# Attention and MLP on one core: the first loads of x, keys and wq divided anew over the SP and ACT queues

## The chip, the core and the metric

One core of one Trainium2 chip. The metric is device microseconds of one execution. The profile's span runs from the first to the last instruction and is about 1.8 us shorter than that time (1236.3 us for a run of 1238.15 us). "Us" in the text is microseconds from the start of the span unless a duration is meant.

## The reference, cut to what matters

```python
def reference(A_x, A_k_cache, A_v_cache, A_wq, A_wo, B_x, B_w1, B_b1, B_w2, B_b2):
    xn = layernorm(A_x)                                  # 2048 x 512, bf16
    q = (xn @ A_wq)                                      # 32 heads of 128
    p = softmax(einsum("bhqd,bhkd->bhqk", q, k_cache) * 128 ** -0.5)
    s = einsum("bhqk,bhkd->bhqd", p, v_cache) @ A_wo
    h = relu(xn @ B_w1 + B_b1) ** 2                      # 512 -> 1792
    g = silu(h @ B_w2 + B_b2)
    return A_x + s * g
```

## The kernel before

TensorE works almost without a break for 1220 us. Nothing of that can begin before four small things have happened: a tile of x (128 rows) has been normalized, transposed and projected to queries of head 0, and the keys of head 0 have been transposed. The kernel therefore starts with loads on two queues, SP's and ACT's, and a hand-ordered beginning.

The loads before the change (`AC` is ACT; a load without a queue goes to SP):

```python
    t_x0 = S.emit_dma(AC, partial(_dma, out=x_ln[P // 2:P, 0, :], in_=A_x[0, P // 2:P, :]), sl_x0)
    t_xl[0] = S.emit_dma(SP, partial(_dma, out=x_ln[0:P // 2, 0, :], in_=A_x[0, 0:P // 2, :]),
                         sl_xl[0])          # x tile 0 in two halves of 64 rows
    ln_load(0, 1, AC)                       # x tile 1, 128 KB, rows of 1 KB
    load_k0(0)                              # first keys: half of head 0's, 256 KB, rows of 2 KB
    fill_wq(0, AC)                          # head 0's wq, 128 KB, rows of 256 bytes
    load_k0(1)                              # second keys
    ...
    ln_load(0, 2, SP); ln_load(0, 3, SP); fill_wq(1); load_v0(0); load_v0(1)
    fill_k(1); fill_wq(2); fill_v(1); load_w1(0)
    for i, k in enumerate([2, 3, 12, 18, 26, 34]):
        at(k, partial(load_w1, i + 1))      # the other w1 loads, at step k of the attention
```

The order of the beginning. Every engine runs its own part of this list in this order:

```python
    warm_up(36)            # TensorE: 36 matmuls on zeros
    k0_transpose(0)        # TensorE: 8 transposes of the first keys
    k0_copy(0)             # ScalarE: copy of the result
    ln_bn(0, 0)            # VectorE: statistics of x tile 0
    ln_rstd(0, 0, eng=DV)  # VectorE, then POOL: the scale factor of tile 0
    ln_bn(0, 1)            # VectorE: statistics of x tile 1
    ln_scale(0, 0)         # VectorE: tile 0 scaled (xn_t)
    first_transpose(0)     # TensorE: tile 0's transposes
    k0_transpose(1)        # TensorE: 8 transposes of the second keys
    bias_rows()
    k0_copy(1)
    ln_rstd(0, 1, eng=DV)
    first_copy(0)
    bias_copy()
    first_proj(0)          # TensorE: queries of head 0 for tile 0
    ln_scale(0, 1)
    first_evac(0)
    first_transpose(1)
    gen_scores(0)          # TensorE: the first scores
    ...                    # cut: from here on TensorE has work all the time
```

The softmax here doesn't subtract the row's maximum and nothing guards it: scores larger than these inputs give would overflow.

## Time and profile before

| | |
|---|---|
| median of the first 3 runs | 1238.32 us (1238.1 to 1238.4) |
| all 42 runs of this kernel | median 1238.49 us; 35 below 1239, mean 1238.44; 7 from 1239.25 to 1240.57 |
| TensorE busy | 1231.2 of 1236.3 us |
| first scores start | 8.05 us |
| x tile 1 lands, first keys land | 5.10, 4.71 us |

The prediction below shows the lines of this profile. They are read so: in a timeline row, start and duration, engine, line, operation, what it writes `<-` what it reads, number of instructions merged; in brackets how long the engine was idle before and what ended that. In the chain of work that ended last there are start, duration and what the end of the execution hung on at that time.

### The profile page before, as it was taken

The page shows a single profiled execution, that of the slowest core. Times are in us where ns is not written, and L with a number is a line of the kernel's source. Part 1 is how long each engine was busy: PE and PEld are TensorE (multiplying, and loading weights), DVE is VectorE, ACT ScalarE, POOL GpSimd, SP SyncE. Part 2 cuts the span into 40 slices and gives each one's busy share as a digit, 9 for nine tenths or more (in the row PEclk, how much of TensorE's full clock was granted, in tenths as well). Part 3 has the DMA queues.
Part 4 walks back from the last instruction along what each step waited for, and adds up shares of the span by engine and source line. Part 5 has one row for each costly group of instructions (what it writes and reads, how often), then busy time and mean ns, then how long its engine had stood idle before and what let it go on. Part 6 is the DMA issues. An engine that isn't in the chain of part 4 may idle for free.

```text
span 1236.3 us, 26936 instructions
## 1 busy us (share of the span) xinstructions
PE 1231.2 (100%) x11885; PEld 818.7 (66%) x11885; DVE 472.5 (38%) x953; ACT 1053.7 (85%) x1044; POOL 31.9 (3%) x73
## 2 busy tenths in 40 slices
PE   9999999999999999999999999999999999999999
PEld 7666666666666666666666666666666666666666
DVE  4453323244435332334444532333344333324333
ACT  7888888888888888888888888888888888888885
POOL 1010000000002000000000200000000000000000
PEclk9999999999999999999999999999999999999999
DMA  9999997777879797878779978788779799878771
GB/s 213 203 243 194 186 178 134 131 143 142 141 151 170 143 160 129 138 140 144 133 133 170 172 138 144 141 148 133 133 145 148 146 154 158 137 134 147 146 123 31
DMA packets 686884, 185.41 MB, mean 150 GB/s; under 512 B 673552, under 2 KB 685584, under 8 KB 686768
## 3 DMA queue, kind: packets, MB, share of 16 engines
q1 hardware_dynamic: 684592, 179.56, 80.8%
q0 software_dynamic: 1424, 3.81, 1.3%
q8 instruction: 94, 1.54, 0.5%
q10 hardware_dynamic: 752, 0.33, 0.1%
q14 instruction: 22, 0.18, 0.1%
HBM read 96.60 MB, written 2.10 MB: 80 GB/s over the span
## 4 chain that ended last, share of the span: by engine, by line
PE 99%; DVE 0%; DMA 0%; ACTq 0%; issue 0%; DVEq 0%
PE psO L157 38%; PE psA L152 36%; PE psF L152 25%; DMA x_ln<-in_A_x_dram 0%; PE psA L157 0%; DVE out_t L165 0%; PE psF L196 0%; DVE tmp_t L175 0%; PE psO L152 0%; DVE st_t L200 0%; DVE xn_t L171 0%; ACTq L208 0%; PE psO L196 0%; DVE xnT L179 0%; DVE b1f L179 0%
## 5 line engine op out<-in xcount | busy, mean ns | idle before, releaser
L161 ACT ACTIVATE pT<-psA 128x1024 bf16<-128x1024 f32 x1024 | 1043.5, 1023 | 163.6 <-PE psA L152 118.3
L157 PEld LDWEIGHTS psO<-v_sb,pT 128*128 128x128 bf16 x8192 | 547.9, 98 | 240.2 <-issue 12.5
L157 PE MATMUL psO<-v_sb,pT 128*128 128x129 bf16 x8192 | 631.2, 220 | 0.0
L152 PE MATMUL psA<-qt_sb,kT 128*128 128x512 bf16 x2032 | 604.4, 379 | 0.0
L179 DVE COPY o_un<-psO 128x258 f32<-128x258 f32 x256 | 97.3, 421 | 399.6 <-PE psO L157 398.9
L152 PE MATMUL psF<-xnT,wq_sb 128*128 128x512 bf16 (+1 forms) x520 | 168.8, 374 | 0.1
L152 PE MATMUL psF<-wo_all,oT 128*128 128x512 bf16 x480 | 163.6, 379 | 0.0
L152 PEld LDWEIGHTS psA<-qt_sb,kT 128*128 128x128 bf16 x2032 | 157.0, 98 | 0.0
L179 DVE CAST qt_sb<-psF 128x512 bf16<-128x512 f32 (+1 forms) x130 | 87.9, 676 | 97.1 <-PE psF L152 97.1
L165 DVE TENSOR_TENSOR o_bf<-o_un,rden 128x512 bf16<-128x512 f32 x128 | 88.6, 692 | 4.6 <-DVE rden L183 0.3
L152 PEld LDWEIGHTS psF<-xnT,wq_sb 128*128 128x128 bf16 x520 | 50.3, 98 | 59.8 <-DVE xnT L179 0.2
L171 DVE TENSOR_SCALAR r_t<-psF,b1f 128x512 bf16<-128x512 f32 x56 | 42.0, 750 | 117.5 <-PE psF L152 117.5
L152 PEld LDWEIGHTS psF<-wo_all,oT 128*128 128x128 bf16 x480 | 46.9, 98 | 56.4
L152 PE MATMUL psF<-xnT,w_sb 128*128 128x512 bf16 x224 | 77.1, 379 | 0.0
L152 PE MATMUL psF<-w_sb,h2T 128*128 128x512 bf16 x224 | 74.1, 379 | 0.0
L152 PEld LDWEIGHTS psF<-w_sb,h2T 128*128 128x128 bf16 x224 | 21.9, 98 | 26.4
L152 PEld LDWEIGHTS psF<-xnT,w_sb 128*128 128x128 bf16 x224 | 21.9, 98 | 26.4
L165 DVE TENSOR_TENSOR z_t<-psF,b2bc 128x512 f32<-128x512 f32 x16 | 11.1, 692 | 67.2 <-PE psF L152 67.2
L165 DVE TENSOR_TENSOR acc<-psF,acc 128x512 f32<-128x512 f32 x28 | 19.3, 688 | 30.0 <-PE psF L152 30.0
L208 POOL DMA_DIRECT2D out_dram<-out_t x12 | 6.7, 555 | 891.0 <-DVE out_t L165 891.0
L165 DVE TENSOR_TENSOR h2T<-r_t 128x512 bf16<-128x512 bf16 x56 | 23.8, 425 | 1.9
L183 DVE RECIPROCAL rden<-o_un 128x4 f32<-128x4 f32 x128 | 22.9, 179 | 4.4
(47 smaller groups left out, 164.3 us busy)
## 6 DMA issues: line engine op xcount, KB each, us to landing
v_sb<-in_A_v_cache_dram SPq DMA_DIRECT2D x127, 512.0 KB, 4.7
wq_sb<-in_A_wq_dram SPq DMA_DIRECT2D x127, 128.0 KB, 3.0
wo_all<-in_A_wo_dram SPq DMA_DIRECT2D x4, 1024.0 KB, 6.3
w_sb<-in_B_w_dram SPq DMA_DIRECT2D x14, 256.0 KB, 4.6
oT<-o_bf SPq DMA_TRANSPOSE x128, 3.9
x_t<-in_A_x_dram POOLq DMA_DIRECT2D x16, 128.0 KB, 3.6
kT<-in_A_k_cache_dram SPq DMA_TRANSPOSE x127, 4.5
x_ln<-in_A_x_dram SPq DMA_DIRECT2D x14, 128.0 KB, 4.2
```

The lines of the kernel that those rows point to most:

```text
L152: return e.matmul(out, lhsT, rhs, start=start, stop=stop)
L157: return e.matmul(out, lhsT, rhs, start=start, stop=stop, skip_group_check=True)
L161: return e.activation(out, in_, func, bias=bias, scale=scale)
L165: return e.tensor_tensor(out, in0, in1, op)
L171: return e.tensor_scalar(out, in0, scalar1=scalar1, scalar2=scalar2, op0=op0, op1=op1)
L179: return e.tensor_copy(out, in_)
L183: return e.reciprocal(out, in_)
L208: return e.dma_start(out, in_)
```

## The change

The intent: x tile 1, which the chain of work waits for, gets the place right behind tile 0 on SP; the first keys move to ACT in its stead; head 0's wq follows the second keys on SP.

```diff
-    def load_k0(b):
+    def load_k0(b, eng=SP):
...
-            SP, partial(_dma, out=kT[:, NSL - 1, b * n * P:(b + 1) * n * P],
+            eng, partial(_dma, out=kT[:, NSL - 1, b * n * P:(b + 1) * n * P],
...
-    ln_load(0, 1, AC)
-    load_k0(0)
-    fill_wq(0, AC)
+    ln_load(0, 1, SP)
+    load_k0(0, AC)
     load_k0(1)
+    fill_wq(0)
```

## The prediction

> **What bounds the kernel now.** I first read the busy shares on the page, then the chain of work that ended last, then busy time by stretch, and only then the first 8 us instruction by instruction.
>
> ```profile
> PE 1231.2 (100%) x11885; PEld 818.7 (66%) x11885; DVE 472.5 (38%) x953; ACT 1053.7 (85%) x1044; POOL 31.9 (3%) x73
> ...
> PE 99%; DVE 0%; DMA 0%; ACTq 0%; issue 0%; DVEq 0%
> ```
>
> TensorE is busy 1231.2 of 1236.3 us, and 99% of the chain is its own. The stretches say where it isn't:
>
> ```profile
> 0.00:8.05 8.05, 5.92 (x66) 5.18 (x66) 3.58 (x12) 3.50 (x4) 3.16 (x14) 1.00 0.80 202
> 8.05:20.00 11.95, 11.88 (x177) 10.23 (x176) 5.50 (x17) 9.78 (x12) 2.08 (x5) 1.00 1.10 215
> 20.00:620.00 600.00, 600.00 (x5748) 396.56 (x5747) 232.88 (x467) 516.16 (x511) 12.49 (x28) 1.00 0.87 159
> 620.00:1220.00 600.00, 600.00 (x5792) 398.26 (x5790) 223.25 (x446) 522.47 (x519) 11.66 (x24) 1.00 0.80 142
> ```
>
> Columns: stretch, length, then PE, PEld, DVE, ACT and POOL busy, granted clock, DMA share, GB/s. From the first scores at 8.05 us to 1220 us, TensorE is never out of work for more than 0.07 us in all. The change touches only the first 8 us, where 8.05 - 5.92 = 2.1 us lie idle (and 3.65 us of the "busy" are warm-up matmuls on zeros). So the question is only when the stream of scores starts; a shift there should reach the end one to one. The chain up to there:
>
> ```profile
> 0.73 0.58 ACTq L208
> 1.31 0.04 issue
> 1.35 3.75 DMA x_ln<-in_A_x_dram
> 5.10 0.02 issue
> 5.12 0.69 DVE st_t L200
> 5.81 0.33 DVE xn_t L171
> 6.14 0.05 issue
> 6.19 0.40 PE psF L196 x4
> ```
>
> Columns: start, us, what. The load is x tile 1, issued second on ACT, landing at 5.10. Its statistics hold up tile 0: VectorE runs in program order, the statistics of tile 1 stand before the scaling of tile 0 (xn_t), and the scale factor was there already:
>
> ```profile
> 4.46 0.57 POOL L165 TENSOR_TENSOR rstd<-ve_t,mhalf 128x1 f32<-128x1 f32 x1 [1.75 <-DVE ve_t L171]
> 4.75 0.45 PEld L196 LDWEIGHTS psO<-ident,kT 128*128 128x128 bf16 x8 [0.30 <-DMA kT<-in_A_k_cache_dram]
> 4.76 0.62 PE L196 MATMUL psO<-ident,kT 128*128 128x128 bf16 x8
> 5.12 0.69 DVE L200 BATCH_NORM_STATS2 st_t<-x_ln 128x6 f32<-128x512 bf16 x1 [0.75 <-DMA x_ln<-in_A_x_dram]
> ```
>
> POOL is done at 4.46 + 0.57 = 5.03; the scaling of tile 0 starts at 5.73. That 0.7 us is all that an earlier tile 1 can give before POOL is the limit.
>
> **What the Trainium skill says.** "Perfetto Trace Analysis", section "DMA Instruction — HWDGE (DVE, Sync)": the descriptor generator (DGE) is one block shared by the issuing sequencers, locked for exclusive use, and the profiled time of an issue includes the wait for the lock. The trace agrees in part: x tile 1's issue on ACT took 0.85 us beside 0.56 for the keys issued at the same moment on SP, but other issues overlap. "DMA: Bandwidth & Descriptors", section "Issuing engines are not separate DMA queues": loads from SP and ACT run on the same 16 engines and interleave, so dividing them saves only issue time. So the number of queues is not the gain here; the order is. The same page, section "Queues, rings and completion order": each engine takes turns between its queue rows, packet by packet. That would let x tile 1 share with the keys from the start, and the trace contradicts it. Packets in 2.8 to 3.4 us, then 3.4 to 3.8 us:
>
> ```profile
> q1 hardware_dynamic: 55, 0.11, 86.7%
> ...
> q1 hardware_dynamic: 45, 0.08, 60.0%
> q10 hardware_dynamic: 14, 0.01, 19.0%
> ```
>
> q1 is SP's row, q10 ACT's. ACT's row is empty from 2.8 to 3.4 although x tile 1 was issued at 1.35 and its 0.85 us issue was over at 2.20: its descriptors came only after those of the first keys. "PSUM — Partial Sum Buffer", section "Engine vs sequencer instructions": the VectorE queue is strict FIFO. The trace agrees: the scaling of tile 0, ready at 5.03, waits until the statistics are through at 5.73.
>
> **The change part by part.** No byte, no instruction is added or removed; three transfers change queue.
>
> 1. x tile 1: from second on ACT to second on SP, still issued near 1.36. The 256 KB of the first keys, issued on SP at 1.36, started packets at about 2.5 and hold the generator nearly 1 us; tile 1's packets began at about 3.45 and landed 1.65 us later. On SP I expect it to have the place that the keys had: packets from 2.5, and landing near 2.5 + 1.65 = 4.15 (estimate). The statistics can then start at 4.21 + 0.15, about 4.38, and are through near 5.0; the scaling is then limited by POOL's 5.03, so starts at 5.07 instead of 5.73: 0.66 us.
>
> 2. First keys (half 0): from second on SP to second on ACT, behind x tile 1 in the generator. Landed at 1.36 + 3.4 = 4.75. Half the bytes of the keys (128 against 256 KB) now go ahead, worth about half of the keys' 0.97 us: +0.4 (estimate), 5.1 to 5.2. The eight key transposes stand before tile 0's transposes in TensorE's order and take 0.45 us of issue (their row above). So tile 0's transposes start at the later of 5.07 + 0.46 = 5.53 (the trace has 5.73 to 6.19) and 5.15 + 0.45 = 5.60, instead of 6.19: 0.6 us. ScalarE's first copy of the keys moves from 5.42 to about 5.8, its second starts at 6.8 instead of 7.07. No cost.
>
> 3. Second keys: stay on SP as its third load, with the same bytes ahead of them over both queues, so landing as before at 1.98 + 3.8 = 5.8. Their transposes ran at 6.42; now they are wanted at about 5.83. Just in time.
>
> 4. Head 0's wq: from ACT (issued 2.23, landed 2.23 + 4.4 = 6.6) to SP behind the keys, issued near 2.4. It is in front of x tiles 2 and 3 and no longer takes turns with them, so 6.4 to 6.6. The first projection started at 7.19, with 0.57 us from the copy xnT (6.62) to it; at 6.60 it now finds wq barely there. I take 0 to 0.1 us as lost.
>
> 5. x tiles 2 and 3, wq 1 and the values are issued one issue (0.43 us) later on SP, but they queue for DMA anyway (x tile 2 took 4.4 us from issue to landing), so they land as before within 0.2 us. Tile 2 (6.8) is wanted at 7.2, wq 1 (7.7) at 8.5, the first values (3.87 + 5.1 = 9.0) at 9.77 - 0.6 = 9.15: the last has only 0.15 us to spare, and may cost 0 to 0.2 us.
>
> 6. ScalarE has one load issue less (0.45 us), so its 1.28 us table load starts near 2.3 instead of 2.71 and ends near 3.6. Off the path: the first copy waits for TensorE.
>
> Sum: -0.6 from steps 1 and 2, +0.05 for wq, +0.05 for values: about -0.5 us, or 0.04% of 1238.32. Predicted 1237.8 us.
>
> **The rivals.** (a) ACT wins the tie. Both queues issue near 1.35, and the keys won on SP although ACT's issue began 10 ns earlier, so SP seems preferred. If the keys on ACT go first after all, x tile 1 again lands at 5.1 and nothing changes: 1238.3. (b) ACT's row itself is slow. Tile 1's late packets could be the second load on ACT being late for its own sake, not standing behind the keys. Then the keys get that lateness: 2.1 us from issue to first packets and about 1.9 us to the end, landing at 5.5 to 5.8, and the keys take the place of x as the wait: tile 0's transposes at 6.0 to 6.2, a gain of 0 to 0.2, so 1238.1 to 1238.3. For it: ACT's half of tile 0 also began later (0.25 us behind SP's). Against it: the empty row in 2.8 to 3.4 fills just when the keys' first engines are through. (c) wq or values become the new bound, wholly: each could swallow up to 0.3 us, result 1238.0. (d) All is hidden: if something else fed TensorE later, the shift would be lost. Against it: no idle of any size between 8.05 and 1220 us, and ScalarE has 0.60 us of idle before the first exponentials.
>
> **Range and chances.** Chain limit at best: 1238.32 - 0.7 = 1237.6; steps as worked out 1237.8; rivals a and b 1238.3; keys later than in b could make it worse by 0.2 or so. The three runs differ by 0.3 us among themselves, half of which I add on each side. Range 1237.3 to 1238.6. A change of 2% would be 25 us, three times the whole start, so faster 0.01, same 0.98, slower 0.01.
>
> **What would show it.** Right: the first wait of VectorE for the second load falls from 0.75 us to nearly 0; statistics of tile 1 at about 4.4; the scaling at 5.1, released by POOL; the key transposes at 5.1 to 5.2; tile 0's transposes at 5.6; the first scores at about 7.5 instead of 8.05; and the rest of the span unchanged. ACT's row empty until about 3.0 and then filled with 2 KB packets. Wrong: tile 1 still near 5.1 (rival a); keys past 5.3 with TensorE waiting for them (rival b); the first projection or the first value matmuls waiting for a DMA (rival c); first scores earlier but the end unchanged (rival d). A difference of more than 1 us would mean that something outside the start moved.

## The result, and the profile after

The median of 6 runs is 1238.28 us (1237.81 to 1240.16), against 1238.30 for 6 runs of the kernel before. The ratio of the fast runs is 1.0001, with a 95% interval of 0.9988 to 1.0014: the same. (A ratio here is the mean time of one kernel's fast runs over that of the other's of the same rounds, so not quite the ratio of the quoted medians.) Leaving out the upper group, which had 2 of the 6 runs after and 1 of the 6 before, the means are 1238.09 and 1238.25.

The chain of work that ended last, of the changed kernel, its first 8 us (start, duration, what):

```profile
1.34 4.60 DMA kT<-in_A_k_cache_dram
5.94 0.05 issue
5.99 0.62 PE psO L196 x8
6.61 0.22 PE psF L196 x4
```

Where the chain before had x tile 1 until 5.10, it now has the first keys until 5.94. The timeline of the changed kernel shows both sides of it:

```profile
3.62 0.69 DVE L200 BATCH_NORM_STATS2 st_t<-x_ln 128x6 f32<-128x512 bf16 x1 [3.62 <-DMA x_ln<-in_A_x_dram]
...
4.63 0.68 DVE L200 BATCH_NORM_STATS2 st_t<-x_ln 128x6 f32<-128x512 bf16 x1
4.81 0.57 POOL L165 TENSOR_TENSOR rstd<-ve_t,mhalf 128x1 f32<-128x1 f32 x1 [2.10 <-DVE ve_t L171]
5.41 0.41 DVE L171 TENSOR_SCALAR xn_t<-x_ln,mv_t,rstd 128x512 bf16<-128x512 bf16 x1
...
5.99 0.62 PE L196 MATMUL psO<-ident,kT 128*128 128x128 bf16 x8 [0.99 <-DMA kT<-in_A_k_cache_dram]
...
8.30 1.05 PE L157 MATMUL psA<-qt_sb,kT 128*128 128x128 bf16 x16
```

The same two steps of TensorE in the kernel before (tile 0's transposes, first scores):

```profile
6.19 0.40 PE L196 MATMUL psF<-ident,xn_t 128*128 128x128 bf16 x4 [0.81 <-DVE xn_t L171]
...
8.05 1.05 PE L157 MATMUL psA<-qt_sb,kT 128*128 128x128 bf16 x16
```

The wanted part happened: the statistics of tile 1 no longer wait for their load (the second line has no bracket), and the scaling of tile 0 starts when POOL is through, at 5.38. It comes at 5.41 instead of 5.73. But TensorE waits for the keys until 5.99, and tile 0's transposes stand behind them. The first scores start at 8.30, a quarter of a microsecond later than before. From there to the end every weight load of TensorE is 0.25 us later than its counterpart of the kernel before, and the profiled run took 1238.41 us, 0.26 more than the one of before.

So this one profile shows a loss of a quarter of a microsecond, and the runs of the lower group a gain of 0.16 us. Both cannot be the whole story; what differs from run to run had to be found.

### The profile page after: what moved, and what is told of

The parts are those of the page before. It is cut to its first block, busy times and chain, and to the rows that moved or that the text cites. A ratio compares the mean times of both kernels' runs of the same rounds, so it can differ in the third digit from the quotient of the medians.

```text
span 1236.6 us, 26729 instructions
## 1 busy us (share of the span) xinstructions
PE 1220.5 (99%) x11678; PEld 818.6 (66%) x11885; DVE 472.3 (38%) x953; ACT 1053.5 (85%) x1044; POOL 31.9 (3%) x73
## 4 chain that ended last, share of the span: by engine, by line
PE 98%; issue 1%; DMA 0%; DVE 0%; ACTq 0%; DVEq 0%
PE psO L157 38%; PE psA L152 35%; PE psF L152 25%; DMA kT<-in_A_k_cache_dram 0%; PE psA L157 0%; DVE out_t L165 0%; PE psF L196 0%; PE psO L196 0%; DVE tmp_t L175 0%; PE psO L152 0%; ACTq L208 0%; DVE xnT L179 0%; DVE xn_t L171 0%; DVE b1f L179 0%; PE psA L196 0%
## 5 line engine op out<-in xcount | busy, mean ns | idle before, releaser
L152 PE MATMUL psA<-qt_sb,kT 128*128 128x512 bf16 x1840 | 563.0, 379 | 10.1
L152 PE MATMUL psF<-xnT,wq_sb 128*128 128x512 bf16 (+1 forms) x508 | 165.7, 374 | 0.3
```

The lines of the kernel that those rows point to most:

```text
L152: return e.matmul(out, lhsT, rhs, start=start, stop=stop)
```

## The experiments

Twelve runs followed, the changed kernel once more and eleven new ones. Kernels are compared only within the same rounds. Since each profile is one execution, I kept a table of the same few moments for all of them (the sections below refer to it; times in us, "L" and "U" count runs of the lower and the upper group):

| kernel | first keys: queue, landed | x tile 1 landed | tile 0 scaled | first scores | profiled run | L / U | before in the same call, mean of L |
|---|---|---|---|---|---|---|---|
| before | SP, 4.71 | 5.10 | 5.73 | 8.05 | 1238.15 | 35 / 7 | |
| changed | ACT, 5.94 | 3.90 | 5.41 | 8.30 | 1238.41 | 4 / 2 | 1238.25 |
| changed, again | ACT, 4.92 | 3.61 | 5.16 | 7.65 | 1238.19 | 5 / 0 | 1238.49 |
| all on SP | SP, 5.73 | 3.95 | 5.00 | 9.23 | 1239.33 | 2 / 3 | 1238.49 |
| both keys on ACT | ACT, 5.73 | 4.14 | 5.45 | 8.44 | 1238.54 | 4 / 1 | 1238.49 |
| before, scaling first | SP, 4.73 | 5.14 | 5.28 | 8.18 | 1238.28 | 4 / 1 | 1238.49 |
| changed, w1 later | ACT, 6.05 | 3.74 | 5.42 | 8.41 | 1238.55 | 3 / 2 | 1238.53 |
| before, w1 later | SP, 4.75 | 5.11 | 5.75 | 8.23 | 1238.34 | 4 / 1 | 1238.53 |
| changed, 18 warm-ups | ACT, 5.93 | 3.75 | 5.29 | 9.43 | 1240.36 | 0 / 5 | 1238.53 |
| changed, x first | ACT, 5.25 | 3.76 | 5.30 | 8.05 | 1238.16 | 5 / 0 | 1238.53 |
| second keys wait | ACT, 4.69 | 3.60 | 5.15 | 9.86 | 1240.54 | 0 / 4 | 1238.48 |
| whole tiles | SP, 4.36 | 3.57 | 5.20 | 7.74 | 1237.85 | 5 / 0 | 1238.48 |
| whole tiles, wq on ACT | SP, 5.41 | 3.60 | 5.25 | 8.22 | 1238.32 | 5 / 0 | 1238.48 |
| whole tiles, w1 early | SP, 4.11 | 3.27 | 5.27 | 7.98 | 1238.09 | 5 / 0 | 1238.40 |

A first reading: in 11 of these 14 rows, the profiled run is the first scores plus 1230.10 to 1230.14 us. What the start loses or wins does reach the end, one to one. The three exceptions (changed again, 18 warm-ups, second keys wait) are explained below.

A "row" is one queue's share of the DMA engines, as in the prediction: q1 is SP's, q10 ACT's. My theory A: the keys on ACT's row take turns with packets of SP's row, and whichever of the 16 DMA engines starts late pays for that. Rivals: B, the descriptor generator, not the row, is the limit; b of the prediction, ACT's row is slow of itself; C, one late engine by chance.

### The changed kernel a second time (after_again)

No edit. Expected:

> The changed kernel unaltered, for a second look and more times. In its first profile the first keys, issued on ACT at 1.34, landed at 5.94, although all but 6 of their packets had started by 4.70: one engine was late. Theory A (the keys on ACT's row take turns with the second keys on SP's row on whichever engine starts late, so this is how the order behaves): keys land again at 5.5 to 6.0, first scores at 8.1 to 8.3, time 1238.2 to 1238.4. Rival C (one engine was late by chance in that one run): keys land at about 5.1, tile 0's transposes at about 5.85, first scores near 7.75, time near 1237.9.

Measured: median 1238.03 us of 5 runs, all in the lower group, against 1238.58 for before (ratio 0.9994, interval 0.9981 to 1.0006). The keys landed at 4.92, not 5.94, and the first scores started at 7.65. So the same kernel gives quite different starts, and the first profile was not the only way it goes. That alone would favour C; the later experiments decide it. By the first-scores rule this run should have taken 7.65 + 1230.1 = 1237.75 us; it took 1238.19. Comparing weight load by weight load with the kernel before shows why: each is 0.40 us earlier, up to 27 us, and none after it. The timeline of TensorE's weight loads there, first the second look at the changed kernel:

```profile
27.00 0.10 PEld L152 LDWEIGHTS psF<-xnT,wq_sb 128*128 128x128 bf16 x1 [0.74 <-DMA wq_sb<-in_A_wq_dram]
```

and the kernel before:

```profile
26.79 0.10 PEld L152 LDWEIGHTS psF<-xnT,wq_sb 128*128 128x128 bf16 x1
```

This is the wq of head 4. In the kernel before it landed at 26.28 and was wanted at 26.79, so it was 0.50 us early and left no trace in any view of waits. (Below, this load as a second limit on the start is "theory D".) In this run it landed at 26.96 and was wanted 0.4 us earlier, and the whole gain of the start was given back in that wait.

### All of the keys on SP (all_on_sp)

```diff
     ln_load(0, 1, SP)
-    load_k0(0, AC)
+    load_k0(0)
     load_k0(1)
     fill_wq(0)
```

> The changed kernel with the first keys back on SP, third there behind x tile 1 and in front of the second keys, so both halves of the keys stand in one row and don't take turns. Theory A (turns between the two rows delay the keys' late engine): keys land at 5.1 to 5.4, the scaling of tile 0 at about 5.4 stays (x tile 0 lands near 3.6 as in the changed kernel), tile 0's transposes at 5.85, first scores 7.7 to 7.8, time 1238.0. Rival B (the generator is the limit, whatever the row): the keys are issued 0.6 us later than on ACT, and land at 5.9 to 6.2, first scores 8.2 to 8.5, time 1238.4 to 1238.6. Rival C (chance): as A.

Measured: median 1239.33 us (ratio 1.0001, 0.9987 to 1.0014). Keys at 5.73, issued at 2.22: late, a little short of what B gave (5.9), and A's 5.1 to 5.4 was wrong. The keys were issued 0.88 us later than on ACT. But from their first packet (3.31) to landing they also took 2.42 us with no packet on ACT's row, where the kernel before took 2.12: taking turns with another row can't explain that, and theory A leaves it open. And 3 of 5 runs are in the upper group, and the profiled one is among them, with first scores at 9.23. TensorE's timeline of this kernel shows why:

```profile
0.98 4.02 PE L152 MATMUL psA<-warm 128*128 128x128 bf16 x36 [0.98 <-POOL mhalf L187]
5.78 1.03 PE L196 MATMUL psO<-ident,kT 128*128 128x128 bf16 x8 [0.78 <-DMA kT<-in_A_k_cache_dram]
...
7.04 1.06 PE L196 MATMUL psO<-ident,kT 128*128 128x128 bf16 x8
```

Eight transposes take 1.03 us here and 0.62 us in the kernel before: from matmul to matmul it is 107 ns instead of 56, until about 9.2 us. The Trainium skill names a cause, "TensorE: Matmul & The Clock Gate", section "Part 1: The HAM clock gate (the "warmup" mystery)": TensorE's clock starts at half rate and is released after a busy window of about 3.4 us, and the window runs free of the kernel's start. The 107 and 56 ns of these traces are the figures that the section gives, and the clock records in the traces change at the same moments as the spacing: the first release is at 4.09 us in the kernel before, from 3.92 to 5.71 in the other profiles with 36 warm-ups, and at 9.22 in this one, where TensorE had idled 0.78 us. Such a gap does not always cost that: the next kernel had one of 0.77 us and the changed kernel one of 0.99, with full pace after both. What decides it was not tested.

### Both halves of the keys on ACT (keys_both_act)

```diff
     load_k0(0, AC)
-    load_k0(1)
+    load_k0(1, AC)
```

> The changed kernel with the second keys also on ACT, behind the first ones; SP has x tiles and wq alone. Theory A: the first keys take turns only with wq's 256-byte packets, cheap ones, so they land at 5.1 to 5.4; second keys at 5.8 to 6.2; first scores 7.7 to 7.9; time 1238.0. Rival b of the prediction (ACT's row is slow of itself, whatever SP's row carries): first keys at 5.8 or later again, second keys later than 6.3, first scores 8.3 or later, time 1238.4 or more.

Measured: median 1238.54 us (ratio 0.9999, 0.9987 to 1.0012); first keys at 5.73, second at 6.79, first scores at 8.44. These are close to the numbers of rival b (5.8 or later, 6.3 or later, 8.3 or later). A had said that 256-byte packets are cheap to take turns with; if A is right at all, that part of it was wrong. This experiment could not tell A from b, since SP still had packets for the same engines all the time.

### The kernel before with tile 0 scaled first (scale_first)

```diff
-    ln_bn(0, 1)
     ln_scale(0, 0)
+    ln_bn(0, 1)
```

> The kernel before, its loads untouched, with only the program order of two VectorE instructions swapped: scaling of tile 0 first, then the statistics of tile 1. If the chain of the kernel before was read rightly (tile 0 held only by the order), the scaling starts at 5.07 instead of 5.73, tile 0's transposes at 5.5 instead of 6.19, its first projection at about 6.65 (wq lands at 6.6); tile 1's statistics start at 5.4 and end at 6.1, so tile 1's scaling is at about 7.05 (7.27 before) and the first scores at 7.6 to 7.85 instead of 8.05: time 1237.9 to 1238.1. Rival: the keys or wq take the place of the wait, first scores at 8.0 and time 1238.3.

Measured: median 1238.28 us (ratio 0.9997, 0.9985 to 1.001); first scores at 8.18. The reading of the chain was right: with the loads untouched, the scaling of tile 0 waits only for POOL now. VectorE's timeline of this kernel:

```profile
5.28 0.41 DVE L171 TENSOR_SCALAR xn_t<-x_ln,mv_t,rstd 128x512 bf16<-128x512 bf16 x1 [0.69 <-POOL rstd L165]
5.61 0.69 DVE L200 BATCH_NORM_STATS2 st_t<-x_ln 128x6 f32<-128x512 bf16 x1
...
7.37 0.41 DVE L171 TENSOR_SCALAR xn_t<-x_ln,mv_t,rstd 128x512 bf16<-128x512 bf16 x1
```

Tile 0's transposes started at 5.75 instead of 6.19. The gain did not come through: tile 1's statistics are now the later ones (5.61 instead of 5.12), so tile 1 is scaled at 7.37 instead of 7.27, and its transposes stand before the first scores in TensorE's order. The rival named keys and wq for that; by the chain that ended last it was tile 1, though TensorE also waited 0.34 us for head 0's wq here, which landed at 7.26 instead of 6.62.

### The second and third w1 loads later (after_w1_later, before_w1_later)

In the changed kernel and, as a control, in the kernel before:

```diff
-    for i, k in enumerate([2, 3, 12, 18, 26, 34]):
+    for i, k in enumerate([10, 11, 14, 18, 26, 34]):
```

> The changed kernel with the second and third w1 loads moved behind head 4's wq in SP's order. In the second look at the changed kernel every weight load was 0.40 us earlier than in the kernel before, up to 27.00 us, where TensorE waited for head 4's wq (landed 26.96) and the whole 0.4 us was given back. Theory D (that load is a second limit on the start): now it lands by 25.8, the slack there is over 1 us, no shift is given back, and the span follows the first scores one to one (first scores + 1230.1 us is the time); 7.65 would give 1237.75, 8.3 would give 1238.4. Rival: other waits take it back, or the loads moved are late themselves: time 0.2 us or more above that sum.

> Control: the kernel before with the same two w1 loads moved. Its slack at head 4's wq was 0.50 us, so theory D expects the slack to grow to about 1.5 us and no gain: within 0.1 us of the kernel before among the lower runs. Rival: if w1 later frees the DMA row for the start as such, it gains 0.2 us or more.

Measured: 1238.55 us for the changed kernel (ratio 1.0003, 0.999 to 1.0015) and 1238.34 for the one before (1.0001, 0.9988 to 1.0014). Head 4's wq landed at 24.76 and 24.68, as expected, and was early by 2.38 and 2.29 us instead of 0.44 (first profile of the changed kernel) and 0.50. The control's profile has no gain (first scores at 8.23, later than in the first profile of before, and 1238.34 us). Its lower group of 4 has a mean 0.22 us under that of before's 8, more than the 0.1 expected, which with so few runs I take for noise and not for a finding. For theory D the first of the two was inconclusive: its profiled start was late (keys at 6.05), so there was no gain that could have been given back.

### 18 warm-up matmuls instead of 36 (after_warm18)

```diff
-    warm_up(36)
+    warm_up(18)
```

> The changed kernel with 18 warm-up matmuls instead of 36. Of 15 runs of the kernel before 3, and of 11 of the changed one 2, were 1.3 to 2 us slower than the rest, and the profile of all_on_sp, in that upper group, has TensorE at half pace (107 ns from matmul to matmul of 128 columns, not 56) until about 9.2 us; in the other profiles full pace came between 4.1 and 5.8. Theory E (upper group = executions in which TensorE reaches full pace late, because it idled before): with 18, TensorE is idle from about 2.9 to 5, full pace comes after 8 us nearly always, first scores at 8.3 to 9.2 and nearly all runs at 1239.0 to 1240.5. Rival (the upper group has another cause, for instance slow memory): share of slow runs stays at a fifth, and the median at 1238.0 to 1238.4.

Measured: median 1239.77 us (ratio 1.0009, 0.9996 to 1.0021), and all 5 runs from 1239.18 to 1240.36: all in the range of the upper group. TensorE's timeline:

```profile
0.98 2.10 PE L152 MATMUL psA<-warm 128*128 128x128 bf16 x18 [0.98 <-POOL mhalf L187]
5.98 1.03 PE L196 MATMUL psO<-ident,kT 128*128 128x128 bf16 x8 [2.90 <-DMA kT<-in_A_k_cache_dram]
...
9.43 0.72 PE L157 MATMUL psA<-qt_sb,kT 128*128 128x128 bf16 x5
```

After 2.9 us of idleness the transposes run at half pace, and full pace came at about 11.5 us (clock record: 11.48); the first scores, at 9.43, were a little later than the 9.2 expected. This is also why this run took 1230.93 us after its first scores and not 1230.1: the first scores were run at half pace too. So a late release of the clock makes an execution as long as the upper group's. For the other kernels this cause is shown in the one execution that was profiled in the upper group (all on SP). For the rest it is likely, not shown, but the lists of runs support it: of the 6 upper runs of the kernel before whose clock is listed, 4 have a mean granted clock of 0.999, and none of the 30 lower ones. What such a figure can be is seen in second keys wait below: a fall to half clock for 3.41 us after the first release.

### A candidate: x first, more warm-up, w1 later (all_three)

```diff
-    warm_up(36)
-    k0_transpose(0)
-    k0_copy(0)
+    warm_up(40)
...
     first_transpose(0)
+    k0_transpose(0)
+    k0_copy(0)
     k0_transpose(1)
```

with the w1 loads as above.

> A candidate that should beat both: the changed kernel, with w1's two loads moved as above, tile 0's transposes ahead of the first keys' (so late keys hold up only the scores), and 40 warm-up matmuls. Tile 0 scaled at 5.1 to 5.4, its transposes at 5.5 to 5.7 whatever the keys do, first projection at 6.7 to 7.1, first scores at 7.4 to 7.8, nothing given back: 1237.5 to 1237.9, that is 0.4 to 0.8 under the kernel before, and fewer runs in the upper group. Rival: wq of head 0 or the keys' copy on ScalarE takes the place of the wait, first scores 8.0, 1238.1.

Measured: median 1238.27 us, 1237.94 to 1239.05 (ratio 0.9999, 0.9985 to 1.0013). Tile 0's transposes started at 5.77 as hoped, but the first scores at 8.05. The two rounds of key transposes, 0.9 us of TensorE's time, which in the kernel before are half done before tile 0 is ready, now all lie between tile 0 and its projection (7.10). No better than before.

### The second keys wait for the first (second_keys_wait)

This kernel is meant to be slower. It adds one wait, so that SP's row is empty while the first keys are on their way on ACT's:

```diff
-    load_k0(1)
+    load_k0(1, deps=[t_k0[0]])     # all later loads on SP wait behind it
     fill_wq(0)
```

> The changed kernel with one wait added: SP issues the second keys, and all loads after them, only when the first keys on ACT have landed, so ACT's row has the DMA engines to itself from about 3.4 us. In the five profiles with the first keys on ACT and the second on SP they landed at 5.94, 4.92, 6.05, 5.93 and 5.25; on SP, in the three profiles with the order of before, at 4.71 to 4.75. Theory A (ACT's last engines take turns with SP's packets): the last packet of the first keys ends by 4.6 and they land by 5.0. Rival b (ACT's row slow of itself): they land again at 5.3 to 6.0. The time itself gets worse, since second keys and wq come some 1.5 us later: 1239.5 to 1240.5.

Measured: median 1241.05 us (ratio 1.002, 1.0006 to 1.0033), half a microsecond above the range given: the second keys came at 7.75, and TensorE, idle for 1.78 us before them, fell back in pace (eight transposes took 0.62 us at 4.74 and 0.93 at 7.80; the clock record has half clock from 7.96 to 11.37), which is also why this run doesn't follow the first-scores rule. The question was the landing of the first keys: 4.69. DMA packets by row, of the changed kernel in 4.4 to 6.0 us (packets, MB, share of 16 engines; q1 is SP's row, q10 ACT's):

```profile
q1 hardware_dynamic: 812, 0.50, 101.2%
q10 hardware_dynamic: 19, 0.03, 4.5%
```

In this kernel, in 3.4 to 4.4 us, and then in 4.4 to 6.0 us:

```profile
q10 hardware_dynamic: 110, 0.19, 56.4%
...
q1 hardware_dynamic: 20, 0.04, 19.1%
```

With nothing on SP's row the keys' last packet starts before 4.4, and ACT's row is empty afterwards. With SP's row full, most of the keys are through at the same time, but 19 packets and completion marks of some late engines are left, and they take turns with 812 others. In the trace of the changed kernel the last packets on ACT's row start 160 ns apart (4.63, 4.79, 4.95, 5.11), where one packet takes 84 ns. So ACT's row is not slow of itself: rival b falls. Traffic on SP's row delays the keys. That it does so by turns is read from this spacing; the experiment took away SP's bytes and the generator's work for them as well, so it doesn't separate A from a generator that serves two queues at once.

The packets also show what the landing alone hides. In the kernel before, the first keys' first packet starts at 2.59 and the landing follows 2.12 us later; here, behind x tile 1 and alone, it is 3.03 and 1.66; in the five profiles with this order of loads, on average 3.07 and 2.56. So the place behind x tile 1 did cost some 0.4 us, as the prediction estimated, and 4.69 is so near to 4.71 only because being alone gave it back. What stays a matter of chance is how late the last engine is: 4.92, 5.25, 5.93, 5.94 and 6.05 in five profiles with this order of loads.

### Whole tiles, keys alone behind them (whole_tiles, whole_wq_act, whole_w1_early)

The Trainium skill, "DMA: Bandwidth & Descriptors", section "Rules for kernel authors", advises against two transfers to disjoint halves of the partitions and for one transfer to 128. So this candidate loads tiles 0 and 1 whole, one first on each queue, and leaves ACT's row empty afterwards:

```diff
-    sl_x0 = S.slot("x0b")
-    t_x0 = S.emit_dma(AC, partial(_dma, out=x_ln[P // 2:P, 0, :], in_=A_x[0, P // 2:P, :]), sl_x0)
-    t_xl[0] = S.emit_dma(SP, partial(_dma, out=x_ln[0:P // 2, 0, :], in_=A_x[0, 0:P // 2, :]),
-                         sl_xl[0])
-    ln_load(0, 1, SP)
-    load_k0(0, AC)
+    t_x0 = None
+    ln_load(0, 0, SP)
+    ln_load(0, 1, AC)
+    load_k0(0)
     load_k0(1)
     fill_wq(0)
```

with w1's loads later and 38 warm-ups. In the second kernel `fill_wq(0, AC)`; in the third, w1's loads where they were.

> A candidate: x tile 0 in one piece first on SP, x tile 1 in one piece first on ACT, both halves of the keys and wq on SP, w1's two loads later, 38 warm-up matmuls. ACT's row is empty after x tile 1, so nothing takes turns with the keys. Generator order: tile 0, tile 1, keys: keys start packets near 3.0 and land at 5.1 to 5.3 like those of before plus 0.48 us for the 128 KB more ahead of them; tile 0 lands at 3.3 to 3.6, tile 1 at 3.6 to 3.9; tile 0 scaled at 5.1 to 5.3, its transposes at 5.6 to 5.8, first scores at 7.5 to 7.8, lower runs at 1237.6 to 1237.9. Rival: keys as in all_on_sp at 5.7, first scores 8.2, no gain.

> The same with head 0's wq second on ACT instead of behind the keys on SP. Theory A: wq's packets now take turns with the keys' on the 16 engines and go ahead of the second keys: first keys 0.1 to 0.5 us later than in whole_tiles (5.3 to 5.7) or the second keys at 6.2 to 6.5 instead of 5.9; wq lands near 6.0 instead of 6.6, which nobody needs; first scores 0.1 to 0.4 us later. Rival (rows don't matter, only bytes): equal within 0.1 us.

> whole_tiles with the two w1 loads back where the kernel before has them, ahead of head 4's wq. In whole_tiles TensorE wanted that wq at 26.48 and it had landed at 24.78. Theory D: with the w1 loads ahead it lands at 26.3 to 27.0 as in the four kernels that had that order (26.28, 26.60, 26.96, 26.92), so if the first scores come at 7.7 again, TensorE waits 0 to 0.5 us for it at 26.5, and time is 0.1 to 0.4 us over the first scores + 1230.1; if the first scores come at 8.1 or later, no wait. Rival: the wait in the second look at the changed kernel was chance, the wq lands by 26.0 and the time is first scores + 1230.1.

Measured: whole tiles 1237.99 us (1237.85 to 1238.19; ratio 0.9994, 0.9982 to 1.0007); with wq on ACT 1238.10 (1237.64 to 1238.54; 0.9995, 0.9981 to 1.0009); with w1 early 1238.14 (1237.96 to 1238.16; 0.9996, 0.9982 to 1.001). Between the first two, TensorE's timelines differ in one thing. Whole tiles:

```profile
5.01 0.76 PE L196 MATMUL psO<-ident,kT 128*128 128x128 bf16 x8
5.67 0.40 PE L196 MATMUL psF<-ident,xn_t 128*128 128x128 bf16 x4
...
7.74 1.05 PE L157 MATMUL psA<-qt_sb,kT 128*128 128x128 bf16 x16
```

With wq on ACT's row:

```profile
5.46 0.62 PE L196 MATMUL psO<-ident,kT 128*128 128x128 bf16 x8 [0.74 <-DMA kT<-in_A_k_cache_dram]
5.92 0.39 PE L196 MATMUL psF<-ident,xn_t 128*128 128x128 bf16 x4
...
8.22 1.05 PE L157 MATMUL psA<-qt_sb,kT 128*128 128x128 bf16 x16
```

The same bytes, one load of 128 KB moved to the other row, and the keys land at 5.41 instead of 4.36 and the scores start half a microsecond later. In the third kernel, with wq on SP again, they landed at 4.11. The keys' first packet hardly moved (2.56 against 2.65); from it to landing it was 2.85 us instead of 1.72, with wq's packets moving on ACT's row meanwhile. That agrees with theory A and corrects my first version of it: 256-byte packets are not cheap to take turns with. Two limits: it is one profile of each kernel, and the other queue also issued wq earlier (1.16 instead of 2.12), so the row and the earlier request are not told apart.

The keys came earlier than I had expected (5.1 to 5.3). The SP issue of tile 0, first in the kernel before and then with whole tiles, has a part in that:

```profile
0.72 0.58 SPq L208 DMA_DIRECT2D x_ln<-in_A_x_dram  x1
```

```profile
0.73 0.40 SPq L208 DMA_DIRECT2D x_ln<-in_A_x_dram  x1
```

Half a tile took 0.58 us to issue and a whole one 0.40. The keys were issued at 1.19 instead of 1.36, and the first packets of all moved at 1.75 instead of 2.08 (first packets in the traces), and the keys' own first packet at 2.65, not near 3.0 as expected. In its issue this agrees with the skill's advice; tile 0 itself landed no sooner whole (3.38 to 3.45) than in halves (3.17 to 3.38 with the order of before). Why the halves are slower to issue no run here shows.

The third kernel was to test the wait for head 4's wq. That landed at 26.53 as expected, was wanted at 26.72 and so was early by 0.18 us: no wait in this profile, whose start was at 7.98. The limit is near, as D says, but the giving back itself was seen in one execution only, the second look at the changed kernel.

Whole tiles is the best of the 13 kernels by median: its mean of 1238.01 is 0.47 us under the mean of the lower group of before on the same chip. All 15 runs of these three kernels are in the lower group; so are the 5 of the candidate with 40 warm-ups, and all other kernels had 36 or 18. Whether two more warm-ups alone do that was not tried. By the interval it is still "same": 0.04% is less than these rounds can tell from nothing, upper group included.

## Why the prediction was right or wrong

The time, 1238.28 us, lay in the range of 1237.3 to 1238.6, and "within 2%" was right. Neither says much for the reasoning: the range also holds the 1238.32 of the kernel before, so no change at all would have lain in it. The predicted gain of 0.5 us was not there, or not most of the time. By its steps:

- **What bounds the kernel.** Right. The start reaches the end one to one (first scores plus 1230.1 us in 11 of 14 profiles), and it was order, not work, that held tile 0 (scaling first: 5.28 instead of 5.73).
- **Step 1, x tile 1.** Right in kind, and tile 1 came even earlier than the 4.15 worked out: 3.90, 3.61, 3.74, 3.75 and 3.76 in the profiles of the changed order, so rival a did not come. The scaling of tile 0 was limited by POOL as said, but at 5.16 to 5.42 instead of 5.07, since tile 0 itself landed later than the 3.17 of the kernel before (3.27 to 3.52 in the five profiles). Whether tile 1's packets caused that is open: profiles with the order of before had 3.17 to 3.38.
- **Step 2, first keys.** This is the step that failed. The prediction put "Half the bytes of the keys (128 against 256 KB) now go ahead, worth about half of the keys' 0.97 us: +0.4 (estimate), 5.1 to 5.2". The mean of five profiles is 5.62, so the step was +0.9, and it varies from +0.2 to +1.3. The term that was counted was about right: the keys' first packet starts at 3.07 on average instead of 2.59, +0.5. The term that was left out is the time from there to landing, 2.56 on average instead of 2.12, another +0.4, and nearly all of the spread: the company of the second keys and wq, one row over, on the same 16 engines. Without that company it was 1.66.
- **Rival b** named the wait that came, and nearly its number (5.5 to 5.8), for the wrong reason. The empty ACT row from 2.8 to 3.4 in the kernel before fits the generator's order, as it was read; that packets of two rows then share the engines by turns, as the Trainium skill says ("DMA: Bandwidth & Descriptors", section "Queues, rings and completion order"), was taken as contradicted when it was merely not yet begun.
- **Step 4 and rival c.** wq of head 0 and the values held nothing in the two profiles of the changed kernel: the first projection and the first value matmuls show no wait for a DMA. The values landed at 9.34 and 9.11 instead of 8.94, later than the 0.2 us allowed in the first of the two, but were wanted later still.
- **Rival d, hidden later.** Held for unlikely on the ground that TensorE had no idle time between 8.05 and 1220 us. That ground was no ground: head 4's wq was 0.50 us early in the kernel before, and a load that is just in time shows no idle time. In the second look it took back all of 0.4 us.
- **Not foreseen:** the release of TensorE's clock, which comes at a different time in each execution and can make 1 to 2 us of difference when TensorE idles before it. It outweighs everything that this change moves.

What stays open: how often the changed kernel gains. Its 9 lower runs in two calls have a mean of 1238.06 us, before's 12 in the same calls 1238.39; that is 0.3 us in its favour (and 0.3 with the upper groups left in: 1238.41 against 1238.72), at ratios of 1.0001 and 0.9994 whose intervals contain 1.

## What to carry to other kernels

Before you value an earlier start, follow the loads that come after it and note how early each one is, not only which ones are waited for: the smallest of these margins caps the gain. The load that everything waited for came soonest here (4.11 and 4.36 us) with little else on the DMA engines and what may follow it behind it in its own row; a second queue beside it did not bring it sooner, it let others share the engines with it. And where an effect is half a microsecond, profile the same kernel twice before believing either profile.

## What the Trainium skill lacked or had wrong

- "Perfetto Trace Analysis", section "DMA Instruction — HWDGE (DVE, Sync)", counts the wait for the generator's lock into the profiled time of an issue. A long second issue (0.85 us in the kernel before) does not by itself show such a wait: with the keys all on SP, SP's second issue took 0.81 us though ACT's only load had been issued by then (1.27 us against 1.36).
- "DMA: Bandwidth & Descriptors", section "Issuing engines are not separate DMA queues", says that several queues save only issue time. It lacks that they can cost time: with one load of 128 KB given to the other queue, and so issued earlier, the 256 KB of keys landed at 5.41 instead of 4.36 us (one profile each).
- The same page, section "Rules for kernel authors", advises one transfer of 128 partitions instead of two of 64, but gives no number for the issue: here 0.58 us for 64 rows of 1 KB and 0.40 us for 128.
- "TensorE: Matmul & The Clock Gate", section "Part 1: The HAM clock gate (the "warmup" mystery)", puts the spread of the release at some 500 ns. Here it came at 3.92 to 5.71 us with 36 warm-ups from 0.98 on, and at 9.22 and 11.48 us in two kernels where TensorE had idled 0.8 and 2.9 us. Before the first release the clock column of these profiles shows 1.00 too, and only the spacing of matmuls tells; a fall after it is shown (0.58 in 8 to 12 us of second keys wait).
- No page gives a number for how late the last of the 16 engines of one load can be: for the same load in the same kernel the landing ranged from 4.92 to 5.94 us.
